# A fused convolution and SiLU layer on one core: one PSUM bank and the hand-written order of work

## The chip, the core and the metric

The kernel runs on one core of a Trainium2 chip. TensorE multiplies, VectorE and ScalarE work element by element, GpSimd (POOL) does small side work, and SyncE (SP) issues most DMAs. Each engine takes its instructions in program order and waits for the others through semaphores. Products land in PSUM, which has eight banks of 512 float32 columns on each of 128 partitions. The metric is device time in microseconds (us), the median of several runs.

## What is computed

```python
w = softmax(weight)                  # 8 heads, 7 taps each
x_pad = zeros of 6 positions, then x # x: 8 x 4096 x 192, float32
a[b, s, h, :] = sum over k of w[h, k] * x_pad[b, s + k, h, :]
h = a @ w_in                         # 32768 x 192 times 192 x 2048
g = h / (1 + exp(-h))                # SiLU
out = g @ w_out                      # 2048 x 192
```

All operands are float32. A float32 matmul here is two passes: every matmul of the program shows as two weight loads and two matmuls in the trace.

## The kernel before

**Blocks and phases.** The 32768 positions are cut into 32 blocks of 1024 (two halves of 512, which lie on partitions 0 to 63 and 64 to 127). Block 0 is computed plainly (`up_plain`, `down_plain`). From block 1 on, both matrix products use fewer multiplications: sums and differences of operands and of results stand in for some products. A steady block has a P phase (the first product, 75 matmuls of 64x128x512 and the plain chunk) and a D phase (the second product, 48 slots of four 128x32 matmuls each). In the D phase of one block, VectorE prepares the convolution of the next; in its P phase VectorE and ScalarE mostly combine what TensorE has just written.

**The order is a list.** `PLAN` holds the order of all work of one steady block as tokens; `step` turns each into instructions, all pinned to program order, so each engine runs its own tokens in the order of the list. A bar only separates TensorE's tokens. A leading `-` means the previous block, `=` the one before it, `+` the next. `START` is the same for the first blocks, and `finish` ends the last. The tokens, as kind, number, dot, group or index:

- `Pr.g` (TensorE, `product`, L625): product r of group g. It runs in half B of the array (partitions 64 to 127) for r in `ON_B` (0, 1, 2, 4, 5, 6, 11, 14, but not r 14 of group 4), otherwise in half A. The two halves run side by side.
- `L.nk` (TensorE, `plain`, L642): the plain chunk, which is computed without the trick. n = 0 is one product per k, on half A, into one bank. n = 1 is a half-width product on each half, into two banks.
- `Di.je` (TensorE, `out_slot`, L741): slot i of the second product; i = 5 is a quarter as wide. It needs SiLU results and, for i of 2 to 5, the differences t of the same j.
- `u`, `X`, `a`, `b`, `S` (`sums_h`): what reads and combines the chains, below. u and S are on ScalarE (L674, L686), X, a and b on VectorE (L668). `SL` is the plain chunk's SiLU (ScalarE, L691).
- `t.ji` (VectorE, `sum_g`, L709): differences of SiLU results; t.01 needs S3.0 and S1.4, t.03 needs t.01.
- `y`, `x`, `z` (ScalarE copies of accumulator parts, L799, L804, L807) and `M` (VectorE sums, L819): they merge the accumulators of the D phase. `o` transposes (VectorE, L829) and `st` stores (SP).
- for the next blocks: `ld` loads (SP), `i` transposes (VectorE, L464), `ha` sets the halo (POOL copy and two SP DMAs), `v.ki` is tap i of the convolution (ScalarE for i = 0, L495, else VectorE, L498), `sp` spreads it by DMA (SP), `w` forms sums of it (VectorE, L532 and L535).

**Chains and banks.** Within a group, products pile up in three banks, and the partial sums in between are results too, so each must be read before the next product of its chain may be added:

```python
CHAINS = ((5, 2, 6, 1, 0, 14), (3, 9, 7, 4, 8), (12, 10))
QUEUE = (0, 4, 1, 2, 3)
CHAIN_BANKS = ((0, 1, 7, 1, 0), (2, 3, 2, 3, 2), (4, 4, 4, 4, 4))
ACC = (7, 1, 3, 5, 6, 4, 0)
PLAIN_BANKS = (7, 7, 3)
```

The first chain is read after products 5, 2, 6, 1, 0 by u5, u4, u2, u0, u1 and at its end by S3. The second is read after 3, 9, 7, 4, 8 by X2, X4, a5, a1, a0, the third after 12 and 10 by b1 and b5. `CHAIN_BANKS` gives the bank of chain and place of the group in `QUEUE`: the third chain is always in bank 4. X2 and X4 write banks 5 and 6, to which P13 and P11 add. In the D phase `ACC` gives the banks: D0 is in bank 7, D1 in 1, D2 in 3, D3 in 5, D4 in 6, D5 in 4 (read by the four x2 copies). `PLAIN_BANKS` gives the plain chunk's: L.0 whole in bank 7, the first half of L.1 in bank 7 as well, its second half in bank 3; SL.0, SL.1 and SL.2 read them in this order.

So L.1 can begin only when SL.0 has read L.0. VectorE's M1 and ScalarE's y2 read one accumulator (D2's bank), M2 and y1 another (D1's), M3 and x0 (D3's), M4, M5 and x1 (D4's) likewise, the sums on partitions 0 to 95 and the copies on 96 to 127.

Of the kernel before, what the change touches and what calls it, by code (L numbers as in the profile page):

```python
# [17 lines left out]
def kernel(  # L18
# [88 lines left out]
    START = (
        "=dp.37 =v.20 =v.00 =dp.19 =v.10 =dp.5 =dp.10 =dp.42 =dp.36 =dp.27 =dp.44 =dp.14 "
        "=dp.8 =dp.12 =dp.38 =dp.28 =dp.22 =dp.25 =dp.43 =dp.26 =dp.45 -ld.2 =dp.30 =dp.3 "
        "=dp.20 -ld.1 =dp.33 =dp.11 -ld.0 =dp.6 =v.01 =dp.17 =v.21 =dp.15 =v.02 =dp.18 =v.11 "  # L110
        "=v.03 =dp.16 =v.12 =dp.47 =v.04 =dp.0 =v.22 =v.13 =dp.23 =v.05 =dp.32 =v.14 =dp.34 "
        "=v.06 =dp.7 =v.15 =sp.0 =v.23 =dp.21 =v.16 =dp.4 =v.24 =sp.1 =dp.40 =v.25 =dp.39 "
        "=v.26 =go.2 =dp.31 -i.2 =sp.2 =dp.1 -i.1 -i.0 =dp.9 -ha.0 =dp.13 =dp.46 =dp.35 =w.0 "
        "-v.20 =dp.41 -v.10 =w.1 =dp.2 -v.11 =w.2 -L.01 -P5.0 -v.21 -L.00 -P5.4 -u5.0 =w.3 "
        "-L.02 -P2.0 -v.22 -v.12 =dp.24 -u4.0 -v.23 -v.00 =dp.29 -SL.0 =w.5 -u5.4 -P6.0 -P3.0 "
        "=cp.1 =cp.2 -P2.4 -u2.0 -X2.0 -L.12 -u4.4 -L.10 -v.01 =cp.0 -L.11 -P9.0 -P1.0 =o.0 "
        "-SL.2 -P13.0 -P6.4 -u0.0 -X4.0 -v.13 -P3.4 -P0.0 -u2.4 =w.4 -S2.0 -P12.0 -P11.0 "
        "-SL.1 -X2.4 -u1.0 -P7.0 -P5.1 -S4.0 -b1.0 -P9.4 -P1.4 -a5.0 -u5.1 -v.14 -P4.0 -P10.0 "
# [24 lines left out]
        "a5.4 S4.4 P5.2 P3.1 b1.4 u2.1 P4.4 P10.4 u5.2 X2.1 v.16 P2.2 P9.1 a1.4 sp.1 P1.1 "
        "P13.1 u4.2 b5.4 X4.1 P8.4 P6.2 u0.1 +i.1 S1.0 P7.1 P0.1 a0.4 u2.2 S2.1 +i.0 P2.3 "
        "P12.1 u1.1 a5.1 +ha.0 P3.2 P1.2 b1.1 P4.1 u0.2 X2.2 P10.1 u4.3 P11.1 a1.1 P9.2 S0.4 "
        "-M7.0 P6.3 S4.1 P8.1 b5.1 P0.2 u2.3 P13.2 X4.2 +v.20 a0.1 P7.2 P11.2 u1.2 -o.0 S2.2 "
        "P3.3 P1.3 S0.1 a5.2 S4.2 P14.1 P12.2 X2.3 +v.10 u0.3 P9.3 P4.2 b1.2 P10.2 P0.3 X4.3 "
        "P11.3 P7.3 u1.3 b5.2 S0.0 a1.2 P12.3 P14.3 S5.0 a5.3 S1.4 P13.3 -o.2 S3.1 P4.3 b1.3 "
        "S3.3 P8.2 P14.2 a1.3 P10.3 t.00 +v.21"
    )  # L150
    QUEUE = (0, 4, 1, 2, 3)
    CHAIN_BANKS = ((0, 1, 7, 1, 0), (2, 3, 2, 3, 2), (4, 4, 4, 4, 4))

    def pin(ins):
        return tc.keep_in_program_order(ins)
# [37 lines left out]
    x0 = x.flatten_outer_dims()[TB - pad : TB, :].rearrange("t (k c) -> c k t", k=NK)  # L193
# [357 lines left out]
    def rows(t, e):  # L551
        return t[R * e : R * e + R]
# [82 lines left out]
    def plain(b, n, k):  # L635
# [3 lines left out]
        for e in range(2) if n else (0,):  # L639
            cols = slice(e * TB // 2, (e + 1) * TB // 2) if n else slice(0, TB)  # L640
            pin(
                nc.tensor.matmul(  # L642
                    banks[PLAIN_BANKS[n and 1 + e]][:, cols],
                    rows(wr[j] if own == e else ws[j], e)[:, a, k, :],
# [43 lines left out]
    def silu_plain(b, i):  # L688
        cols = slice((i - 1) * TB // 2, i * TB // 2) if i else slice(0, TB)
        h = h_of(b, None, int(i > 0))[:, cols]  # L690
        pin(nc.scalar.activation(h, banks[PLAIN_BANKS[i]][:, cols], AF.Silu))  # L691

# [418 lines left out]
```

## Time and profile before

| what | value |
|---|---|
| median of 3 runs | 2359.12 us (2358.9 to 2359.2) |
| the profiled execution, its own time | 2359.21 us |
| its span, first to last instruction | 2357.4 us, granted TensorE clock 0.999 |
| VectorE and ScalarE busy | 2110.6 us and 1179.4 us |
| one L625 matmul as recorded | 589 ns; its weight load 187 ns |
| one X, a or b on VectorE (L668) | 670 to 690 ns |
| one u on ScalarE (L674) | 589 ns |
| one t on VectorE (L709) | 1220 ns |
| HBM traffic | 31.46 MB read, 25.17 MB written |

[...]The distance between starts tells the pace. Times of single tokens are read off the timeline by counting each engine's instructions along the list, in a block whose D phase begins at 1156.38 us.

### The profile page before, as it was taken

Reading aid. Unit: us, or ns where it says so; the run is one execution under the profiler, and the core shown is the slowest. Engines: PE = TensorE matmul, PEld = TensorE weight load, DVE = VectorE, ACT = ScalarE, POOL = GpSimd, SP = SyncE. Lnnn points to the kernel's source line nnn. Section 1 sums busy time; section 2 is a strip of 40 time slices with the busy share of each in tenths; the row PEclk is TensorE's granted clock in tenths of the full one; section 3 lists DMA queues with packets and bytes.
Section 4 is the critical chain, followed back from the end, with each engine's and each line's share of the span. In section 5 each row is a group of like instructions: output and inputs, shape, how many; then the busy total and the mean of one; then the engine's idle time right before and its main releaser. Section 6 shows DMA issues by size and latency. Waiting matters only on the chain.

```text
span 2357.4 us, 43991 instructions
## 1 busy us (share of the span) xinstructions
PE 2349.2 (100%) x17630; PEld 1043.8 (44%) x17630; DVE 2110.6 (90%) x2877; ACT 1179.4 (50%) x2275; POOL 105.7 (4%) x168
## 2 busy tenths in 40 slices
PE   9999999999999999999999999999999999999998
PEld 4344443444444444444444444444444444444444
DVE  8999989899899999998998999999999989899867
ACT  5345644456544465444564445654446644456443
POOL 4910000000000000000000000000000000000000
PEclk9999999999999999999999999999999999999999
DMA  7232111222112221222221122212222112222111
GB/s 158 51 66 52 37 35 35 52 53 47 26 33 52 53 53 29 38 40 52 53 43 28 35 53 52 52 23 36 48 52 52 36 32 37 52 53 39 21 20 28
DMA packets 451245, 106.56 MB, mean 45 GB/s; under 512 B 423584, under 2 KB 428704, under 8 KB 451040
## 3 DMA queue, kind: packets, MB, share of 16 engines
q1 hardware_dynamic: 447392, 101.78, 23.7%
q8 instruction: 138, 2.26, 0.4%
q0 software_dynamic: 448, 1.58, 0.3%
q10 hardware_dynamic: 3200, 0.39, 0.1%
q14 instruction: 67, 0.55, 0.1%
HBM read 31.46 MB, written 25.17 MB: 24 GB/s over the span
## 4 chain that ended last, share of the span: by engine, by line
PE 99%; DVE 1%; ACT 0%; issue 0%; ACTq 0%; DVEq 0%
PE ps L741 47%; PE ps L625 45%; PE ps L642 2%; PE ps L762 2%; PE ps L570 2%; PE ps L1010 1%; PE ps L422 0%; DVE t L709 0%; DVE g L668 0%; DVE cmb L819 0%; DVE cmb L162 0%; ACT u L162 0%; ACT yx L804 0%; DVE osb L162 0%; DVE win L532 0%
## 5 line engine op out<-in xcount | busy, mean ns | idle before, releaser
L741 PE MATMUL ps<-g,wo 128*32 128x512 f32 x2976 | 691.9, 592 | 0.0
L625 PE MATMUL ps<-win,wr 64*128 64x512 f32 x1550 | 691.3, 595 | 0.0
L625 PE MATMUL ps<-win,ws 64*128 64x512 f32 x1550 | 674.3, 603 | 0.6 <-ACT u L674 0.6
L674 ACT COPY u<-ps 128x512 f32<-128x512 f32 x775 | 445.8, 589 | 184.6 <-PE ps L625 158.0
L741 PE MATMUL ps<-t,wo 128*32 128x512 f32 (+2 forms) x4528 | 536.6, 446 | 0.5 <-DVE t L709 0.5
L741 PE MATMUL ps<-t,wx 128*32 128x512 f32 x2976 | 495.7, 592 | 0.0
L625 PE MATMUL ps<-dup,wr 64*128 64x512 f32 x868 | 423.8, 590 | 0.0
L498 DVE SCALAR_TENSOR_TENSOR nat<-xt,taps,nat 128x512 f32<-128x512 f32 x564 | 415.4, 755 | 5.6 <-ACT nat L495 2.0
L709 DVE TENSOR_TENSOR t<-g 128x1024 f32<-128x1024 f32 x248 | 299.9, 1220 | 61.1 <-PE ps L741 41.0
L709 DVE TENSOR_TENSOR t<-g,t 128x1024 f32<-128x1024 f32 x248 | 302.7, 1221 | 30.0 <-PE ps L741 24.7
L625 PEld LDWEIGHTS ps<-win,wr 64*128 64x128 f32 x1550 | 261.4, 186 | 148.3 <-issue 62.4
L686 ACT ACTIVATE g<-ps 128x512 f32<-128x512 f32 x465 | 275.4, 602 | 83.8 <-PE ps L625 78.0
L668 DVE TENSOR_TENSOR g<-u,ps 128x512 f32<-128x512 f32 x465 | 305.7, 673 | 10.1 <-PE ps L625 1.4
L741 PEld LDWEIGHTS ps<-t,wo 128*32 128x32 f32 x4528 | 185.4, 110 | 274.2 <-issue 270.6
L625 PEld LDWEIGHTS ps<-win,ws 64*128 64x128 f32 x1550 | 242.6, 185 | 144.8 <-issue 49.5
L625 PE MATMUL ps<-dup,ws 64*128 64x512 f32 x682 | 280.9, 602 | 0.0
L668 DVE TENSOR_TENSOR ps<-u,ps 128x512 f32<-128x512 f32 x310 | 214.5, 692 | 69.8 <-PE ps L625 64.0
L686 ACT ACTIVATE g<-g 128x512 f32<-128x512 f32 x465 | 268.4, 633 | 15.3 <-DVE g L668 15.3
L804 ACT COPY yx<-ps 32x512 f32<-32x512 f32 x150 | 84.2, 579 | 380.0 <-PE ps L741 377.6
L741 PE MATMUL ps<-g,wx 128*32 128x512 f32 x1488 | 246.0, 594 | 0.0
L741 PEld LDWEIGHTS ps<-g,wo 128*32 128x32 f32 x2976 | 170.1, 110 | 112.5 <-issue 103.9
L807 ACT COPY cmb<-ps 96x512 f32<-96x512 f32 x30 | 17.5, 583 | 403.8 <-PE ps L741 403.8
(90 smaller groups left out, 1849.2 us busy)
## 6 DMA issues: line engine op xcount, KB each, us to landing
dup<-nat SPq DMA_DIRECT2D x345, 128.0 KB, 2.3
nat<-in_x_dram SPq DMA_DIRECT2D x382, 64.0 KB, 2.4
out_dram<-osb SPq DMA_DIRECT2D x376, 64.0 KB, 2.0
raw<-in_moe_w_out_dram SPq DMA_DIRECT2D x8, 384.0 KB, 3.6
raw<-in_moe_w_in_dram SPq DMA_DIRECT2D x12, 192.0 KB, 4.5
ws<-wr POOLq DMA_DIRECT2D x8, 192.0 KB, 5.0
raw<-in_moe_w_in_dram SPq DMA_DIRECT2D x6, 128.0 KB, 3.0
xt<-xt SPq DMA_DIRECT2D x31, 4.5 KB, 1.9
```

What stands on the lines that cost most here:

```text
L498: nc.vector.scalar_tensor_tensor(out=dst, in0=src, scalar=tap, in1=dst, op0=ALU.mult, op1=ALU.add)
L570: nc.tensor.matmul(hs[a, n, e], rows(wr[j], e)[:, a, k, :], rows(d, e)[:, n, k, :], start=k == 0, stop=k == NK - 1,)
L625: nc.tensor.matmul(to[:, cols], raw(g, *LEFT[e][r], e), rhs[:, cols], start=first, stop=True, skip_group_check=True,)
L642: nc.tensor.matmul(banks[PLAIN_BANKS[n and 1 + e]][:, cols], rows(wr[j] if own == e else ws[j], e)[:, a, k, :], rows(dups[b], e)[:, SLOT[e ...
L668: pin(nc.vector.tensor_tensor(out_, u, v, op=op))
L674: pin(nc.scalar.copy(us[b, g, o][:, cols], t1[:, cols]))
L686: pin(nc.scalar.activation(h, src, AF.Silu))
L709: pin(nc.vector.tensor_tensor(t[i // 2][:, i % 2, :], u, v, op=ALU.subtract))
L741: nc.tensor.matmul(accs[b][at][SQ * q : SQ * q + SQ, to], lhs[:, e, SQ * k : SQ * k + SQ], rhs[:, e, ts(q, TB // 4) if i == 5 else to], st ...
L762: nc.tensor.matmul(banks[DOWN_BANKS[k]][R * n : R * n + R, :], wo[j][:, a, e, R * k : R * k + R], gs[b, j, a][:, n, e, :], start=j == 0 an ...
L804: pin(nc.scalar.copy(to, acc[3 * (name[0] == "x") + k][n:P, :]))
L1010: nc.tensor.matmul(by_pe[k][n], rows(diag, n)[:, k, i, :], rows(xts[0], n)[:, k, i : i + TB], start=i == 0, stop=i == K - 1,)
```

## The change

One entry of `PLAIN_BANKS` changes: the first half of L.1 goes to bank 4, the third chain's bank, in place of bank 7; the definition moves up beside the other banks. `PLAN` and `START` hold the same tokens in another order. In the new order L.1's three products are spread among L.0's, the y, z and x copies stand in other places against the M sums, and o, st, ld, i, ha, sp and v stand elsewhere too. No instruction is added or removed. The whole of `PLAN` follows, and of `START` the places where block 0 ends and the first P and D phases meet.

```diff
@@ -79,77 +79,78 @@
 
 
     PLAN = (
-        "P5.0 | -P8.3 -S3.2 -sp.2 v.00 -t.01 | -D1.31 -S2.3 -S5.2 | -D1.01 -a0.2 -S1.3 =st.2 "
-        "-a0.3 -S1.1 | -D1.11 -b5.3 -S0.2 | -D0.00 -S5.4 v.22 -sp.0 -S4.3 | -D2.01 -t.03 "
-        "-S5.1 -S1.2 | -D0.20 =st.0 -t.02 -S0.3 | -D1.21 -S5.3 v.01 | -D2.00 v.11 | -D5.01 "
-        "+ld.0 | -D0.30 v.02 | -D3.00 -t.10 | -D0.01 +ld.1 v.23 | -D0.31 v.24 | -D4.00 -t.11 "
-        "+ld.2 | -D3.01 -w.0 | -D4.01 | -D0.11 -t.13 | -D2.11 -w.1 | -D5.00 | -D4.11 -t.12 | "
-        "-D5.11 | -D2.10 -t.20 | -D4.10 -t.21 | -D5.10 | -D0.21 | -D0.10 -t.23 | -D3.11 "
-        "-z1.0 v.25 u5.0 | -D4.20 v.03 | -D1.10 -t.22 | -D3.10 | -D4.21 -t.30 | -D1.20 v.12 "
-        "| -D2.20 -t.31 | -D2.21 | -D1.30 -t.32 | -D3.21 -t.33 | -D5.20 | -D2.31 v.04 | "
-        "-D1.00 v.26 | -D4.31 -w.2 | -D2.30 v.05 | -D5.30 -y2.0 | -D3.20 v.06 -y1.0 -M1.0 | "
-        "-D3.31 v.13 | -D3.30 -M2.0 | -D5.31 v.14 -x0.0 | -D4.30 -y0.0 -M3.0 | -D5.21 -x1.0 "
-        "| P2.0 | L.00 -M4.0 -x2.1 -w.3 | L.01 | P5.4 u4.0 -w.4 | L.02 | P6.0 u5.4 v.15 | "
-        "P3.0 | P2.4 SL.0 v.16 u2.0 | L.12 -x2.3 X2.0 | L.11 -x2.2 u4.4 | L.10 -M5.0 | P9.0 "
-        "| P1.0 +i.0 SL.2 SL.1 | P13.0 | P6.4 +i.1 -x2.0 u0.0 X4.0 | P3.4 | P5.1 u2.4 +i.2 "
-        "S2.0 | P7.0 | P0.0 -M6.0 +ha.0 X2.4 | P12.0 | P11.0 u1.0 a5.0 u5.1 | P9.4 | P1.4 "
-        "b1.0 S4.0 | P13.4 | P4.0 u0.4 X4.4 -w.5 | P10.0 | P2.1 a1.0 | P0.4 | P7.4 u4.1 b5.0 "
-        "S2.4 | P11.4 | P8.0 -o.1 u1.4 a5.4 | P6.1 | P12.4 S4.4 a0.0 | P14.4 | P14.0 -M7.0 "
-        "u2.1 S0.0 b1.4 | P4.4 | P3.1 S3.4 +v.10 | P10.4 | P1.1 X2.1 S3.0 a1.4 | P5.2 | P9.1 "
-        "u0.1 | P0.1 | P13.1 u5.2 X4.1 | P2.2 b5.4 | P8.4 -o.3 | P7.1 | P5.3 u4.2 a0.4 -st.3 "
-        "u1.1 | P6.2 | P12.1 S2.1 a5.1 u5.3 | P11.1 | P3.2 -st.1 b1.1 u2.2 S5.0 | P4.1 | "
-        "P10.1 X2.2 S4.1 sp.1 | P2.3 S1.0 | P9.2 a1.1 -o.0 | P1.2 | P8.1 u4.3 X4.2 | P6.3 | "
-        "P13.2 u0.2 a0.1 +v.20 | P11.2 b5.1 | P7.2 u2.3 -o.2 S2.2 | P0.2 | P3.3 S4.2 a5.2 | "
-        "P1.3 | P12.2 u1.2 X2.3 | P4.2 u0.3 | P9.3 b1.2 S0.4 | P14.1 | P10.2 S1.4 X4.3 | "
-        "P0.3 S3.1 | P7.3 b5.2 | P11.3 u1.3 a1.2 | P12.3 S0.1 a5.3 | P14.3 | P13.3 +v.21 | "
-        "P4.3 S3.3 b1.3 | P8.2 a1.3 | P10.3 | P14.2 t.00"
+        "+ld.1 P5.0 | -P8.3 -S1.4 -a0.2 -S4.3 | -D0.00 -t.01 -S0.2 | -D1.00 -S1.2 =o.2 v.00 "
+        "| -D2.01 -t.03 -S5.1 =st.2 | -D2.00 -b5.3 | -D1.20 -sp.0 v.21 -S5.3 | -D4.01 u5.0 "
+        "-t.02 -S1.3 | -D5.01 -sp.2 | -D4.00 -t.10 | -D0.20 -t.11 | -D3.01 | -D0.11 -t.12 | "
+        "-D1.30 v.22 | -D3.00 +ld.2 -t.13 | -D2.11 -a0.3 | -D5.00 | -D2.10 -t.20 -S0.3 | "
+        "-D3.11 v.11 | -D5.10 | -D4.11 -w.0 | -D0.30 v.12 | -D4.10 -t.21 | -D1.11 -t.23 | "
+        "-D0.21 | -D0.01 v.23 -w.1 | -D3.10 -t.22 | -D5.21 | -D0.31 | -D5.11 | -D1.10 -t.30 "
+        "| -D1.01 -t.31 | -D2.20 | -D2.21 v.13 | -D5.20 | -D4.21 v.01 v.14 | -D4.20 v.24 | "
+        "-D1.21 -w.2 | -D3.20 -t.33 | -D2.30 v.02 | -D1.31 -t.32 | -D2.31 -y1.0 | -D5.30 "
+        "v.03 | -D0.10 v.25 | -D3.21 -z1.0 v.15 -y0.0 | -D4.31 -y2.0 -w.3 | -D5.31 -M1.0 | "
+        "-D3.30 -x2.1 v.26 -x2.0 | -D4.30 -x2.2 -M2.0 | -D3.31 -w.5 -x0.0 -M3.0 | L.02 | "
+        "P2.0 -x2.3 -w.4 | P5.4 | P3.0 u4.0 -M6.0 | L.12 v.16 u5.4 | L.00 | P6.0 -x1.0 -M4.0 "
+        "| L.10 u2.0 | P2.4 | L.01 X2.0 | L.11 v.04 u4.4 | P9.0 | P1.0 SL.0 -M5.0 SL.2 | "
+        "P6.4 | P13.0 u0.0 X4.0 SL.1 | P5.1 | P3.4 -M7.0 S2.0 +i.2 u2.4 | P0.0 | P7.0 X2.4 | "
+        "P11.0 | P12.0 u1.0 a5.0 -o.1 | P9.4 | P1.4 S4.0 b1.0 -st.1 u5.1 | P13.4 | P4.0 X4.4 "
+        "u0.4 | P10.0 | P2.1 a1.0 +ld.0 v.05 | P7.4 | P0.4 u4.1 b5.0 | P14.0 | P8.0 u1.4 "
+        "v.06 S5.0 | P11.4 | P14.4 a5.4 S3.0 a0.0 S2.4 | P6.1 | P12.4 S3.4 | P4.4 | P3.1 "
+        "u2.1 b1.4 S4.4 | P5.2 | P10.4 X2.1 | P1.1 a1.4 u5.2 | P9.1 b5.4 | P2.2 u0.1 | P8.4 "
+        "X4.1 | P5.3 u4.2 | P7.1 a0.4 | P0.1 +i.1 u5.3 sp.1 | P12.1 a5.1 | P6.2 u1.1 | P3.2 "
+        "-o.0 | P4.1 u2.2 b1.1 | P13.1 | P2.3 a1.1 | P10.1 S2.1 | P1.2 u4.3 X2.2 | P8.1 | "
+        "P11.1 -o.3 u0.2 | P13.2 S1.1 a0.1 | P6.3 S4.1 | P9.2 +i.0 | P0.2 b5.1 u2.3 +ha.0 | "
+        "P3.3 S0.0 X4.2 | P1.3 S2.2 | P12.2 u1.2 | P11.2 X2.3 | P7.2 u0.3 b1.2 | P14.1 S4.2 "
+        "| P9.3 a5.2 S0.4 | P0.3 -st.0 | P10.2 S1.0 X4.3 | P14.2 u1.3 | P7.3 b5.2 +v.20 "
+        "-st.3 | P4.2 S0.1 | P12.3 a5.3 S3.1 | P14.3 +v.10 a1.2 | P13.3 | P4.3 S5.2 b1.3 | "
+        "P8.2 S2.3 | P11.3 a1.3 S3.3 | P10.3 S5.4 t.00 S3.2"
     )
     START = (
-        "=dp.37 =v.20 =v.00 =dp.19 =v.10 =dp.5 =dp.10 =dp.42 =dp.36 =dp.27 =dp.44 =dp.14 "
...
-        "-v.20 =dp.41 -v.10 =w.1 =dp.2 -v.11 =w.2 -L.01 -P5.0 -v.21 -L.00 -P5.4 -u5.0 =w.3 "
-        "-L.02 -P2.0 -v.22 -v.12 =dp.24 -u4.0 -v.23 -v.00 =dp.29 -SL.0 =w.5 -u5.4 -P6.0 -P3.0 "
...
+        "=dp.28 =v.20 =v.10 =dp.44 =v.00 =dp.18 =dp.6 =dp.40 =dp.7 =dp.32 =dp.23 =dp.30 "
...
+        "=v.26 =go.2 =sp.0 =dp.19 -i.0 =dp.46 -i.2 =dp.31 -ha.0 =dp.9 =sp.2 =dp.4 =dp.41 "
+        "-v.10 -v.00 -v.11 =dp.8 -v.20 -v.01 =dp.5 -v.12 =dp.16 -v.02 =w.0 =dp.10 =w.1 =cp.0 "
+        "-L.01 -P5.0 -v.03 =cp.1 -L.02 -P5.4 =w.2 -u5.0 -L.10 =w.3 -u5.4 -P2.0 -P3.0 -v.13 "
...
+        "-b1.3 -S5.1 ld.0 -S4.3 -t.01 -D0.01 -S5.2 -D0.21 -t.02 -D1.11 -sp.0 -a5.3 -D1.10 "
+        "-v.25 -t.03 -P8.2 P5.0 +ld.1 -P4.3 -P10.3 -D1.30 -b5.3 -v.26 -D1.00 -a0.2 -sp.2 "
...
+        "-D5.11 -D2.10 u5.0 -t.20 -D0.20 -w.1 -D3.11 -t.21 -D4.10 -w.2 -D2.11 -t.23 -P8.3 "
+        "P2.0 -D0.31 -a0.3 -t.22 -D3.10 -S0.3 -S1.3 -D4.21 v.21 -S5.3 u4.0 v.01 -D4.20 -t.30 "
...
+        "P13.3 -o.3 P4.3 S3.2 b1.3 -st.3 +v.10 P8.2 +v.20 a1.3 P10.3 P11.3 S5.2 t.00 S2.3"
     )
     QUEUE = (0, 4, 1, 2, 3)
     CHAIN_BANKS = ((0, 1, 7, 1, 0), (2, 3, 2, 3, 2), (4, 4, 4, 4, 4))
+    PLAIN_BANKS = (7, 4, 3)
 
     def pin(ins):
         return tc.keep_in_program_order(ins)
@@ -599,7 +600,6 @@
     X_OF = {13: 0, 10: 5, 5: 3, 11: 4, 14: 1}
     CHAINS = ((5, 2, 6, 1, 0, 14), (3, 9, 7, 4, 8), (12, 10))
     ACC = (7, 1, 3, 5, 6, 4, 0)
-    PLAIN_BANKS = (7, 7, 3)
     XBANK = {2: 5, 4: 6}
```

## The prediction

> **What bounds the kernel now.** I read the page's busy times and its chain that ended last, then the waits, then single blocks through windows and timeline.
>
> ```profile
> PE 2349.2 (100%) x17630; PEld 1043.8 (44%) x17630; DVE 2110.6 (90%) x2877; ACT 1179.4 (50%) x2275; POOL 105.7 (4%) x168
> ...
> PE 99%; DVE 1%; ACT 0%; issue 0%; ACTq 0%; DVEq 0%
> ```
>
> TensorE is the chain. Whether it runs at its pace, its busy share can't say, so I compare starts. The windows below are one steady block: D phase, P phase, whole block.
>
> ```profile
> 1156.38:1192.60 36.22, 36.22 (x386) 12.09 (x385) 33.06 (x39) 9.51 (x19) 0.00 (x0) 1.00 0.30 52
> 1192.60:1228.76 36.16, 36.16 (x173) 20.04 (x169) 32.63 (x52) 27.36 (x54) 0.63 (x1) 1.00 0.18 34
> ...
> 1156.38:1228.76 72.38, 72.38 (x554) 32.13 (x553) 65.70 (x90) 36.86 (x72) 0.63 (x1) 1.00 0.24 43
> ```
>
> The columns are length, then busy time of PE, PEld, DVE, ACT, POOL, then clock and DMA. The block's 72.38 recurs to 0.01 us from the third block to the last, so a gain or loss per block counts some 29 times. In the P phase each half of the array (A: partitions 0 to 63, B: 64 to 127) has 39 full products of two passes, and passes of one half start 0.4292 us apart (1208.75 and 1209.18 below), and six half-width ones at 0.2155: 33.48 + 1.29 = 34.77. The phase takes 36.16, so 1.39 is lost: 0.10 at the switch to D, 1.29 in stalls on half A (about 1.2 on B, side by side with them). The D phase has no stalls: its starts run at 0.858 per slot, 0.218 for a quarter-width one. Which stalls they are:
>
> ```profile
> DVE cmb L819 <- ACT yx L804: 29.7, 88, 3.0
> ...
> PEld ps L642 <- ACT g L691: 17.9, 30, 0.7
> ```
>
> The second row is L.12, which shares bank 7 with L.0 and waits for SL.0, once a block:
>
> ```profile
> 1195.54 0.60 ACT L691 ACTIVATE g<-ps 128x512 f32<-128x512 f32 x1 [0.29 <-PE ps L625]
> ...
> 1196.19 0.18 PEld L642 LDWEIGHTS ps<-dup,ws 64*128 64x128 f32 x1 [0.59 <-ACT g L691]
> 1196.19 0.48 PE L642 MATMUL ps<-dup,ws 64*128 64x256 f32 x1
> ...
> 1196.51 0.38 PE L642 MATMUL ps<-dup,ws 64*128 64x256 f32 x1
> ```
>
> Silu ends at 1196.14, weights load at 1196.19, the second pass comes 0.32 later in place of 0.2155. With 0.05 at the first pass that is 0.15 us on half A. The other kind, P3.1 -> X2.1 -> P9.1:
>
> ```profile
> 1208.75 0.59 PE L625 MATMUL ps<-dup,ws 64*128 64x512 f32 x1
> ...
> 1209.07 0.70 DVE L668 TENSOR_TENSOR ps<-u,ps 128x512 f32<-128x512 f32 x1 [0.59 <-PE ps L625]
> 1209.18 0.59 PE L625 MATMUL ps<-dup,ws 64*128 64x512 f32 x1
> ...
> 1209.82 0.69 PE L625 MATMUL ps<-win,ws 64*128 64x512 f32 x1
> ...
> 1210.35 0.83 PE L625 MATMUL ps<-win,ws 64*128 64x512 f32 x2
> ```
>
> Half A's passes of P10.4 start at 1208.75 and 1209.18, so P9.1 was due at 1209.61. It may not add to its bank before X2.1 has read it (ends 1209.77): start 1209.82, and its second pass 0.53 later, not 0.43: 0.31 lost. In the same way P10.1 loses 0.26 (behind b1.1), P9.3 0.26 (X2.3), P7.3 0.20 (X4.3). With 0.10 at the first product and L.12's 0.15 that is half A's 1.29 (0.10 + 0.15 + 0.31 + 0.26 + 0.26 + 0.20).
>
> **The rule in it.** From a product's start to the start of its VectorE reader 1.13 us pass, the reader takes 0.69, and 0.05 go to the weight load: 1.87. With one product of the same half between, 1.72 are offered: 0.15 late, and 0.105 for a second pass whose weights could not load beneath the first. That is 0.26. A ScalarE copy (1.06 + 0.59 + 0.05 = 1.70) is just in time and costs only about 0.09, as P6.2, P6.3 and P14.3 show (0.08 each). With two between (2.58) nothing is lost. The block's stalls obey: lost = reader's end + 0.05 + 0.105 - due start, if positive. One more kind: P14.2 loses 0.41 on B because its weight load stands in TensorE's queue behind that of P10.3, which waits for b1.3; a wait on one half can hold up the other.
>
> **The Trainium skill.** "Trainium Kernel Development and Optimization", Performance Expectations, calls matmul busy time "a bad metric" because matmuls are pipelined; the trace agrees (72.38 of 72.38 busy with 1.4 lost). "TensorE: Matmul & The Clock Gate", Part 3, has weight loads overlap running matmuls on other row groups, and be pulled ahead; the halves' matmuls starting 0.01 apart and the exposed 0.105 after a waited load agree. "PSUM — Partial Sum Buffer", PSUM bank collisions, wants engines kept apart by bank and 32-partition quadrant. Copies (partitions 96 to 127) and sums (0 to 95) already wait for each other here (29.7 us above); no run shows a collision. "TensorEngine Tiling (Array Packing)", Key Properties, says that a change of tiling mode drains TensorE; the trace shows 0.09 to 0.2 at each.
>
> **The change part by part.** Counts of every instruction stay; only places and one bank move.
>
> *Bank of L.1's first half.* SL.0 -> L.12 goes: 0.15 on A, 0.04 on B. New are x2 -> L.12 and SL.1 -> P12.0, both on bank 4. x2.3, the last x2, stands on ScalarE behind x0.0 (0.58) and ends some 0.9 us after the last D's results, about 0.8 before L.12 is due. SL.1 ends about 1.2 before P12.0. Both cost nothing. If that cover went, L.12 would delay both halves one for one, with everything behind it on TensorE.
>
> *Links on half A.* With one product of the half between I count 15 links before and 10 after. After, on A: P10.4 behind b1.4, P7.1 behind X4.1, P7.3 behind X4.3, at 0.26 each; P14.4 behind u1.4, 0.09; P9.1 behind X2.1 nothing, since the 0.26 just lost at P10.4 makes its 1.72 into 1.98. P8.1, P8.2 and P8.3 follow P4 of the other half, and A lags B by more than 0.3 there: nothing. With 0.10 at the first product, 0.97. Several readers end within 0.1 of the point (X2.1, b5.2 before P12.3, X2.2 before P13.2, a1.2 before P8.2); I put 0.05 for them: 1.02.
>
> *Half B:* 0.10, P2.2 0.09, P4.1 0.03, P1.3 0.09, and one new wait: P5.0 reopens bank 0, which S3.3 must have read. ScalarE from the start of P0.3: 1.06, u1.3 0.49, v.20 0.62, S0.1 0.52, S3.1 0.52, v.10 0.62, S5.2 0.52, S2.3 0.52, S3.3 0.60 (starts follow at these distances in the trace), together 5.47, and 0.155 to the array: 5.62. Six products of B offer 5.15: 0.47 lost. B's 0.78 stay 0.2 below A's, so A decides. Queued behind P5.0 is only P8.3, then D.
>
> *The seam into D.* S1.4, three Silus after S3.3, ends 7.04 after P0.3's start, t.01 (1.22) at 8.30, D2.01 is due at 8.49: 0.1 us of room, cost nothing. In the list before, S1.4 ran long before t.01.
>
> *Moved on SP, POOL and VectorE.* The halo (ha.0, POOL 0.59, DMA issue 0.62, 1.9 to landing) moves from P0.0 to P0.2; its taker v.20 starts 4.7 us after i.0 ends, 1.6 of room. It passes st.1, ld.0 and sp.1 on SP, all issued earlier. o.2 and st.2 move into the D phase; t.10 takes a buffer that st.2 must have left, and t.10 has 2 us of room. VectorE's D-phase work is 31 us of 36. M3 still stands right behind x0, M4 behind x1: VectorE goes on waiting there, about 0.9 us under D, with X2.0 still done 0.2 before P9.0. So avoiding common reads is worth nothing on TensorE.
>
> *START.* The two products slots dp.24 and dp.29 no longer interrupt the first P phase (two switches, some 0.45 saved); a second stretch of P tokens stands within the first D phase (some 0.25 added). Its other stalls I can't price; the first blocks of the trace lose some 5 us over the steady pace, so +-2.5 is taken, value -0.2.
>
> *Sum.* (1.29 - 1.02) x 29 = 7.8, and 0.2: 8.0 less. The profiled execution is 2359.21 (span 2357.4 and 1.8 around it; 0.1 above the median): **2351.2**.
>
> **Rivals.**
> - *Even (0.22).* The near misses count in full: four on A at up to 0.1. 0.97 + 0.35 is 1.32, as before: 2359. For it: P6.0, P6.2 and P14.3 paid 0.08 with readers done 0.02 ahead. Against: P2.4, 0.05 ahead, paid half.
> - *More gained (0.15).* Stalls of one half hide beneath the lag of the other, as P9.2 and P10.2 show today (one between, nothing lost). If two of the three 0.26 go so: 0.5 per block, 2344.5.
> - *Slower (0.18).* ScalarE's tail at the seam. Late by over 0.2 us there, half B ends last, and D2.01 waits behind t.01 too; beyond 0.2 each us counts, and past 0.45 the gain is gone. At 0.7 the block is 0.23 longer: 6.7 more, 2365.9. For it: eight copies and Silus in a row, ScalarE 27 of 36 us busy in this phase, a halo DMA moved close before v.20. Against: no link in that row waited for in my count.
> - That the change doesn't do what it says: VectorE's waits for copies would remain near 29.7 us. They lie under TensorE; the time stays that of the forecast.
>
> **How the numbers follow.** Forecast 0.45, own range 2347 to 2354.4. About 0.2% (4.7 us) is what can be told from no change. Forecast and more-gained: faster, 0.60. Even: 0.22. Slower: 0.18. Range 2343 to 2365: beneath it the far end of more-gained, above it half of slower.
>
> **What would show it.** Right: block period 72.1, P phase 35.9; no wait of L642 on ACT g L691; P10.4, P7.1 and P7.3 late by 0.26; P5.0 waiting for S3.3 about 0.5 without TensorE's D phase starting later. Wrong: D2.01 behind t.01, half B ending last, or L.12 waiting for a copy of bank 4.

## The result and the profile after

| | before | after |
|---|---|---|
| median of 6 runs each, on one chip | 2359.18 us (2358.9 to 2359.48) | 2349.12 us (2348.82 to 2349.58) |
| ratio after to before, 95% interval | | 0.9957 (0.9945 to 0.997) |
| the profiled execution and its span | 2359.21, 2357.4 | 2349.19, 2347.5 |
| start of the third D phase, from which the blocks are steady | 215.51 | 212.43 |
| from there to the start of the last D phase, 29 blocks | 2098.87 | 2092.12 |
| from there to the end | 43.04 | 42.93 |

Faster by 10.06 us, 0.43%. The spans differ by 9.9: 3.08 come from the first blocks, 6.75 from the steady ones (0.233 in each) and 0.11 from the end.

The page's busy times and the chain that ended last, after:

```profile
PE 2340.3 (100%) x17630; PEld 1061.0 (45%) x17630; DVE 2099.6 (89%) x2877; ACT 1187.3 (51%) x2275; POOL 96.8 (4%) x168
...
PE 99%; DVE 0%; ACT 0%; issue 0%; ACTq 0%
```

TensorE is the whole chain, as before, and the two lines don't tell the kernels apart. The windows of one steady block do (D phase, P phase, block; columns: length, busy time of PE, PEld, DVE, ACT, POOL, clock, DMA share, GB/s):

```profile
1150.31:1186.53 36.22, 36.22 (x386) 12.07 (x385) 33.09 (x40) 8.14 (x17) 0.00 (x0) 1.00 0.20 40
1186.53:1222.45 35.92, 35.92 (x172) 20.62 (x168) 32.19 (x50) 29.01 (x55) 0.19 (x1) 1.00 0.27 47
1150.31:1222.45 72.14, 72.14 (x553) 32.69 (x552) 65.28 (x90) 37.15 (x72) 0.19 (x1) 1.00 0.24 43
```

The D phase has its 36.22 still. All of the gain is in the P phase, 36.16 to 35.92. What was waited for, after (engine, tile, line, releaser: total us, times, longest):

```profile
PEld ps L642 <- issue: 69.4, 218, 0.8
DVE cmb L819 <- ACT yx L804: 61.6, 59, 4.2
PEld ps L625 <- DVE ps L668: 57.8, 214, 0.8
...
PEld ps L625 <- ACT u L674: 15.6, 61, 0.6
```

L642's wait for ACT g L691, L.12 behind SL.0, is gone. VectorE's wait for the copies has doubled, from 29.7 to 61.6: both lists keep a copy and a sum of one accumulator apart by letting the second wait for the first, M1 for y2 (1.21 us in this block) and M3 for x0 (0.77).

The product that lost 0.15 before, L.12, in the timeline of after:

```profile
1187.92 0.19 PEld L642 LDWEIGHTS ps<-dup,ws 64*128 64x128 f32 x1 [0.23 <-issue]
...
1188.35 0.38 PE L642 MATMUL ps<-dup,ws 64*128 64x256 f32 x1
...
1188.57 0.38 PE L642 MATMUL ps<-dup,ws 64*128 64x256 f32 x1
```

Its weights load 0.43 ahead of the first pass, and the second pass comes 0.22 after the first: nothing lost. One of the links that remain, b1.4 -> P10.4:

```profile
1202.10 0.69 DVE L668 TENSOR_TENSOR u<-u,ps 128x512 f32<-128x512 f32 x1 [0.64 <-PE ps L625]
...
1202.84 0.29 PEld L625 LDWEIGHTS ps<-dup,ws 64*128 64x128 f32 x2
1202.84 0.69 PE L625 MATMUL ps<-dup,ws 64*128 64x512 f32 x1
...
1203.38 0.59 PE L625 MATMUL ps<-dup,ws 64*128 64x512 f32 x1
```

b1.4 ends at 1202.79, the weights load at 1202.84 (0.15 late), and the second pass comes 0.54 after the first in place of 0.43: 0.25 lost. And the new wait on half B, S3.3 -> P5.0:

```profile
1219.99 1.08 ACT L686 ACTIVATE g<-ps 128x512 f32<-128x512 f32 x2
...
1221.12 0.18 PEld L625 LDWEIGHTS ps<-dup,wr 64*128 64x128 f32 x1 [0.29 <-ACT g L686]
1221.12 0.69 PE L625 MATMUL ps<-dup,wr 64*128 64x512 f32 x1
```

The first row is S2.3 and S3.3; S3.3 ends at 1221.07. P5.0 starts 0.05 later and had been due 0.29 earlier; with its exposed second load it loses 0.395. D starts at 1222.45 all the same, since half A ends 0.28 after B.

What each product of this block lost, in us (its distance from the one before it of its half, less 0.4292 a pass):

| half | predicted | measured |
|---|---|---|
| A | first 0.10, P14.4 0.09, P10.4 0.26, P9.1 0, P7.1 0.26, P7.3 0.26, near misses 0.05: 1.02 | first 0.104, P9.0 0.047, P14.4 0.127, P10.4 0.254, P9.1 0.011, P7.1 0.265, P7.3 0.262: 1.07 |
| B | first 0.10, P2.2 0.09, P4.1 0.03, P1.3 0.09, P5.0 0.47: 0.78 | first 0.105, P1.0 0.047, P2.2 0.081, P1.3 0.081, P4.3 0.077, P5.0 0.395: 0.79 |

### The profile page after: what moved, and what is told of

It is laid out like the page before. It is cut to its first block, busy times and chain, and to the rows that moved or that the text cites. A ratio compares the mean times of both kernels' runs of the same rounds, so it can differ in the third digit from the quotient of the medians.

```text
span 2347.5 us, 43988 instructions
## 1 busy us (share of the span) xinstructions
PE 2340.3 (100%) x17630; PEld 1061.0 (45%) x17630; DVE 2099.6 (89%) x2877; ACT 1187.3 (51%) x2275; POOL 96.8 (4%) x168
## 4 chain that ended last, share of the span: by engine, by line
PE 99%; DVE 0%; ACT 0%; issue 0%; ACTq 0%
PE ps L741 47%; PE ps L625 42%; PE ps L642 5%; PE ps L762 2%; PE ps L571 2%; PE ps L1010 1%; PE ps L423 0%; DVE t L709 0%; ACT g L686 0%; DVE cmb L163 0%; ACT u L163 0%; DVE osb L163 0%; DVE osb L829 0%; DVE g L668 0%; PE ps L449 0%
## 5 line engine op out<-in xcount | busy, mean ns | idle before, releaser
L625 PE MATMUL ps<-win,wr 64*128 64x512 f32 x1550 | 720.3, 597 | 0.0
L741 PE MATMUL ps<-g,wo 128*32 128x512 f32 x2976 | 702.4, 593 | 0.0
L625 PE MATMUL ps<-win,ws 64*128 64x512 f32 x1550 | 631.3, 595 | 0.0
L741 PE MATMUL ps<-t,wo 128*32 128x512 f32 (+2 forms) x4528 | 545.7, 446 | 0.0
L625 PE MATMUL ps<-dup,wr 64*128 64x512 f32 x868 | 425.4, 593 | 0.0
L686 ACT ACTIVATE g<-g 128x512 f32<-128x512 f32 x465 | 286.1, 633 | 231.5 <-DVE g L668 231.5
L625 PEld LDWEIGHTS ps<-win,wr 64*128 64x128 f32 x1550 | 275.6, 186 | 150.4 <-issue 67.8
L668 DVE TENSOR_TENSOR g<-u,ps 128x512 f32<-128x512 f32 x465 | 311.2, 680 | 28.8 <-PE ps L625 14.6
L625 PE MATMUL ps<-dup,ws 64*128 64x512 f32 x682 | 324.2, 599 | 0.0
L625 PEld LDWEIGHTS ps<-win,ws 64*128 64x128 f32 x1550 | 254.7, 186 | 110.5 <-issue 40.8
L686 ACT ACTIVATE g<-ps 128x512 f32<-128x512 f32 x465 | 266.8, 597 | 41.1 <-PE ps L625 38.4
L668 DVE TENSOR_TENSOR ps<-u,ps 128x512 f32<-128x512 f32 x310 | 214.7, 692 | 43.7 <-ACT g L686 19.0
L741 PEld LDWEIGHTS ps<-t,wx 128*32 128x32 f32 x2976 | 120.5, 110 | 217.5 <-issue 202.3
```

Of the source, the lines that this page charges most:

```text
L625: nc.tensor.matmul(to[:, cols], raw(g, *LEFT[e][r], e), rhs[:, cols], start=first, stop=True, skip_group_check=True,)
L668: pin(nc.vector.tensor_tensor(out_, u, v, op=op))
L686: pin(nc.scalar.activation(h, src, AF.Silu))
L741: nc.tensor.matmul(accs[b][at][SQ * q : SQ * q + SQ, to], lhs[:, e, SQ * k : SQ * k + SQ], rhs[:, e, ts(q, TB // 4) if i == 5 else to], st ...
```

## The experiments

All are lists of the same tokens, or shorter readers, on this kernel. Each ran beside before on one chip; "period" is the usual length of a steady block, 72.375 before and 72.142 after. The lists there take a few lines fewer, so the same code stands up to three lines higher: the L625 of after is L622 or L623, its L668 L665 or L666, and so on.

### The bank alone, in the old order

```diff
-L.00 -M4.0 -x2.1 -w.3 | L.01 | P5.4 u4.0 -w.4 | L.02 | P6.0 u5.4 v.15
+L.00 -M4.0 -x2.1 -x2.0 -w.3 | L.01 | P5.4 u4.0 -x2.2 -w.4 | L.02 | P6.0 u5.4 -x2.3 v.15
...
-L.12 -x2.3 X2.0 | L.11 -x2.2 u4.4
+L.12 X2.0 | L.11 u4.4
...
-PLAIN_BANKS = (7, 7, 3)
+PLAIN_BANKS = (7, 4, 3)
```

The copies of bank 4 go ahead of L.12, in START cp.0 too. In block 1 SL.1 reads after P12.0 has added to its bank, so that block's plain chunk holds other values; no instruction is added or left out.

> The list of before with the new bank alone; the four x2 copies (and, in the first block, one copy of the plain second product) come ahead of L.12, since they read bank 4. Theory (the bank removes SL.0 -> L.12, 0.15 us per block on half A and 0.04 on half B; A falls from 1.29 to 1.14 of stalls, B stays at 1.16): the block 0.12 to 0.15 shorter, 4 us less, 2355 (2354 to 2356). Rival (the gain is the list's alone): 2359.2 within 0.6.

Measured: 2359.71 us, ratio 1.0002 (0.9993 to 1.0011). The forecast of a gain fell. L.12 lost nothing any more, as it said, yet the period is 72.338, only 0.037 less. The timeline shows the next link of the same half, X2.1 -> P9.1:

```profile
1282.43 0.69 DVE L665 TENSOR_TENSOR ps<-u,ps 128x512 f32<-128x512 f32 x1 [0.63 <-PE ps L622]
...
1283.17 0.29 PEld L622 LDWEIGHTS ps<-win,ws 64*128 64x128 f32 x2
1283.18 0.69 PE L622 MATMUL ps<-win,ws 64*128 64x512 f32 x1
```

P9.1 starts 0.05 after X2.1 (1283.12) and loses 0.35 where it lost 0.31 before; P9.0, which lost nothing before, loses 0.08 behind X2.0. So of the 0.15 that L.12 gave back, 0.12 are lost later on half A, at readers that did not come earlier. At the rate of 0.037 the 29 blocks bring 1.1 us. Against this the third D phase starts 0.55 later (216.06), and four blocks (those that end at 360.87, 650.58, 867.93 and 1012.76 us) take 0.13, 0.36, 0.34 and 0.16 more, because VectorE starts one add 0.35 late in each; the last of these experiments comes back to such starts. The bank alone is worth nothing that can be measured; the gain needs the new order. That order in turn needs the bank: it puts L.12 ahead of L.00, and in bank 7 the two products would lie on the same columns.

### The start of before, under the new list

```diff
-a1.3 P10.3 t.00 +v.21
+a1.3 S5.2 S2.3 P10.3 S5.4 t.00 S3.2 +v.21 S1.1 -st.0
```

The new PLAN and bank; START is the old one, with cp.0 ahead of L.12, and closes with the tokens that the new PLAN expects to be done (the diff is against the old START). Block 1's plain chunk is changed as in the run above.

> The changed kernel with the first blocks' list of before, which is closed with the few tokens that the new steady list wants done. Theory (the two traces stand 3.1 us apart when the third D phase begins, and that is kept to the end): 2352.2 (2351.5 to 2353). Rival (what START gains or loses is made up by the blocks behind it): 2349.1 within 0.6.

Measured: 2353.77 us, ratio 0.9977 (0.9968 to 0.9986), 0.8 above the range of the forecast; the rival falls. The period is 72.142, the new one; the difference from after, 4.6 us, is in the first blocks: the third D phase starts at 216.28, and that block takes 0.43 more, where the two lists join. One later block (it ends at 433.49 us) takes 0.35 more, again with one VectorE add that starts 0.35 late (413.99). The old START on its own costs 3.08 (215.51 to 212.43); the other 0.77 up to the third D phase and the 0.43 go with the way it was joined to the new list. Later blocks make up for none of it.

### Half B's new wait taken away

```diff
-P4.3 S5.2 b1.3 | P8.2 S2.3 | P11.3 a1.3 S3.3
+P4.3 S3.3 S5.2 b1.3 | P8.2 S2.3 | P11.3 a1.3
```

> The changed kernel with S3.3 moved ahead of S5.2 and S2.3 on ScalarE, so that P5.0 need not wait (0.40 us lost on half B in the trace of after). Theory (half A ends 0.28 later than B and decides): no change, 2349.1 within 0.7, with P5.0's wait gone in the trace. Rival (ScalarE's tail at the seam decides): up to 0.3 to 0.4 per block, 2338 to 2341.

Measured: 2349.03 us, ratio 0.9956 (0.9941 to 0.9971), period 72.141. P5.0 loses nothing now, and the block is no shorter: half A sets the end of the P phase.

### One more product between P12.4 and P10.4

```diff
-P14.4 a5.4 S3.0 a0.0 S2.4 | P6.1 | P12.4 S3.4
+P12.4 a5.4 S3.0 a0.0 S2.4 | P6.1 | P14.4 S3.4
```

On top of the run before.

> As S3.3 early, and P14.4 and P12.4 exchanged on half A, which gives both links P0.4 -> P14.4 and P12.4 -> P10.4 one more product between. Theory: P14.4's 0.13 and P10.4's 0.25 go, but P9.1, no longer sheltered, pays 0.26: 0.12 to 0.13 less per block on A, while B may lose 0.1 at P5.2 (S3.4 is later) out of its room of over 0.6: 2345.5 (2344 to 2347). Rival (stalls on one half simply move on along it): 2349 within 0.7.

Measured: 2351.95 us, ratio 0.9969 (0.9957 to 0.998): slower than after, above the forecast and above its rival. P14.4 loses nothing now, but the period is 72.246. The timeline:

```profile
1275.29 0.60 ACT L684 ACTIVATE g<-ps 128x512 f32<-128x512 f32 x1 [0.49 <-PE ps L623]
...
1275.94 0.18 PEld L623 LDWEIGHTS ps<-dup,wr 64*128 64x128 f32 x1 [0.70 <-ACT g L684]
1275.94 0.69 PE L623 MATMUL ps<-dup,wr 64*128 64x512 f32 x1
1275.94 0.18 PEld L623 LDWEIGHTS ps<-dup,ws 64*128 64x128 f32 x1
1275.94 0.69 PE L623 MATMUL ps<-dup,ws 64*128 64x512 f32 x1
```

S3.4 follows P14.4 and ends at 1275.89; P5.2 of half B waits for it. The weight load of P10.4 (the one with ws, half A) stands right behind P5.2's in TensorE's queue, so P10.4 starts in the same hundredth and loses 0.149, though b1.4 is long done. P9.1 is then without the shelter that the prediction gave it (0.26 lost just ahead of it) and loses 0.343 in place of 0.011. P7.1 and P7.3 stay at 0.263 each. Half A: 0.10 more, as the period says.

### Shorter readers, on the tight links and on others

```diff
+    SHORT = (("b1", 4), ("X2", 1), ("X4", 1), ("X4", 3), ("b5", 2))
...
-            pin(nc.vector.tensor_tensor(out_, u, v, op=op))
+            n = TB // 2 if (name, g) in SHORT else TB
+            pin(nc.vector.tensor_tensor(out_[:, 0:n], u[:, 0:n], v[:, 0:n], op=op))
```

The five sums named read half their columns. The second kernel names b1.3, X2.3, X4.0, X4.4 and b5.0, which have room. The Trainium skill ("VectorE: DVE Perf Modes", the section on the TRN2 errata) gives (N + 151)/0.96 ns for a float32 add of N columns, which it checked at 512 and 2048; for 256 that is an estimate of 0.42 us. The trace has 0.43 (X4.3, which reads one operand from PSUM), against 0.69 for 512.

> The changed kernel with five VectorE sums (b1.4, X2.1, X4.1, X4.3, b5.2) made on columns 0 to 255 alone, so part of the chains' combination is left out; each stands in a link of half A with one product between. Theory (the link's length is the stall): 0.27 us off each reader, half A's three stalls of 0.26 go, A ends ahead of B, and B (0.74 of stalls, 0.40 of it at P5.0) decides: 0.2 to 0.33 per block, 2339 to 2343. Rival (VectorE's load or TensorE's own pace sets the phase): the same as for the five sums outside tight links, whichever that is.

> The changed kernel with five VectorE sums (b1.3, X2.3, X4.0, X4.4, b5.0) made on columns 0 to 255 alone, so part of the chains' combination is left out; each has two products of its half between. The same time is taken from VectorE as in the run with the tight ones. Theory: nothing, 2349.1 within 0.7. Rival (VectorE's load): as much as the tight ones give, 6 us or more.

Measured: tight 2338.06 us, ratio 0.991 (0.9895 to 0.9925), a little more gained than forecast, period 71.787; loose 2348.65 us, ratio 0.9955 (0.994 to 0.997), period 72.146. VectorE had the same work taken away in both. On five links it brings 0.36 us a block, 11 us in all; elsewhere nothing. So VectorE's load (89% busy in after) is not the bound: single readers are. On half A 0.70 is left of 1.07. Two links that half A's lag behind B had sheltered now show, P8.1 with 0.15 and P8.2 with 0.08. P8.3 loses 0.19 for another reason: it starts 0.01 after P5.0 of half B (1215.67 and 1215.66 us), which waits for S3.3 and whose weight load stands ahead of P8.3's. Half A now ends only 0.01 after B.

### Both together: the tight readers short, S3.3 early

> The five short sums in tight links together with S3.3 early; the same part of the combination is left out. Theory (the later half decides): A's stalls and B's P5.0 are both gone, B has 0.35 and A about 0.3 left, though P8.1, P8.2 and P8.3, which follow products of half B, may now be late on A: 0.45 to 0.7 per block, 2328 to 2336, more than the short sums and S3.3 early give one by one. Rival (effects add up one by one): the time of the short sums within 1 us.

Measured: 2338.06 us, ratio 0.991, no less than with the short readers alone. The forecast fell: this is the rival's number. The windows (D phase, P phase) show where the gain went:

```profile
1216.85:1253.26 36.41, 36.41 (x385) 11.95 (x384) 33.55 (x41) 8.61 (x18) 0.00 (x0) 1.00 0.20 39
1253.26:1288.63 35.37, 35.37 (x172) 20.12 (x168) 30.39 (x50) 28.55 (x55) 0.19 (x1) 1.00 0.27 47
```

The P phase is 0.19 shorter than with the short readers alone (35.56): P5.0 no longer waits, and P8.3's 0.19 is gone with it. The D phase is 0.19 longer than its 36.22. In the timeline of that D phase:

```profile
1217.49 1.22 DVE L709 TENSOR_TENSOR t<-g,t 128x1024 f32<-128x1024 f32 x1
...
1218.77 0.12 PEld L741 LDWEIGHTS ps<-t,wx 128*32 128x32 f32 x3 [0.90 <-DVE t L709]
```

D2.01 waits for t.01, the wait that the prediction's slower rival named. t.01 starts at 0.64 after the D phase's begin, behind a0.2 (which ends at 0.63) and S1.4 (0.60), that is, behind the tails of both VectorE and ScalarE. In after it ends 0.34 before D2.01 starts; here TensorE came to it 0.55 earlier in the block, and the tails did not. That is the next bound: of the 0.55 that the P phase is shorter, 0.36 per block is kept with these tails.

### Sums ahead of copies

```diff
--w.5 -x0.0 -M3.0 | L.02
+-w.5 -M3.0 -x0.0 | L.02
...
-P6.0 -x1.0 -M4.0 | L.10
+P6.0 -M4.0 -x1.0 | L.10
```

> The changed kernel with M3 ahead of x0 and M4 ahead of x1, so that ScalarE's copy waits for VectorE's sum of the same accumulator in place of the other way round. Theory (these waits lie under other work; x2.3 ends just in time for L.12): 2349.1 to 2350. Rival (the order of copies and sums on one accumulator is what the new list gains by): 2 us or more slower.

Measured: 2371.15 us, ratio 1.005 (1.0034 to 1.0067), period 72.877: the largest miss. The D phase is unchanged, P9.0 loses 0.74 and P1.0 0.57. The timeline around P9.0, first of after, then of this run:

```profile
1189.22 0.58 ACT L804 COPY yx<-ps 32x512 f32<-32x512 f32 x1
...
1189.88 0.59 ACT L674 COPY u<-ps 128x512 f32<-128x512 f32 x1
...
1190.57 0.68 DVE L668 TENSOR_TENSOR ps<-u,ps 128x512 f32<-128x512 f32 x1
...
1191.30 0.30 PEld L625 LDWEIGHTS ps<-win,ws 64*128 64x128 f32 x4 [0.18 <-DVE ps L668]
```

```profile
1199.70 0.58 ACT L802 COPY yx<-ps 32x512 f32<-32x512 f32 x1 [0.74 <-DVE cmb L817]
...
1200.30 1.26 ACT L672 COPY u<-ps 128x512 f32<-128x512 f32 x2
...
1200.92 0.70 DVE L666 TENSOR_TENSOR ps<-u,ps 128x512 f32<-128x512 f32 x1 [1.26 <-ACT u L672]
...
1201.67 0.30 PEld L623 LDWEIGHTS ps<-win,ws 64*128 64x128 f32 x4 [0.70 <-DVE ps L666]
```

Top to bottom they are x1, u2.0, X2.0 and P9.0's (and P1.0's) weight loads. M4 comes late on VectorE, behind w.4, M6 and v.16; x1 now waits 0.74 for it on ScalarE, u2.0 stands behind x1, X2.0 needs u2.0, P9.0 needs X2.0. The swap of two readers costs this much only through what is queued behind the one that waits.

### Sums ahead of copies, with nothing behind the copies

```diff
--D4.30 -x2.2 -M2.0 | -D3.31 -w.5 -x0.0 -M3.0 | L.02 | P2.0 -x2.3 -w.4 | P5.4 | P3.0 u4.0 -M6.0 | L.12 v.16 u5.4 | L.00 | P6.0 -x1.0 -M4.0 | L.10 u2.0
+-D4.30 -x2.2 -x2.3 -M2.0 | -D3.31 -w.5 -M3.0 | L.02 | P2.0 -w.4 | P5.4 | P3.0 u4.0 -M4.0 -x0.0 | L.12 -M6.0 u5.4 | L.00 | P6.0 v.16 | L.10 u2.0 -x1.0
```

> The new list, with the sums M3 and M4 ahead of the copies x0 and x1 again, but so that nothing urgent stands behind a waiting copy: x2.3 stands right after x2.2, x0 behind u4.0, x1 behind u2.0, and on VectorE M4 comes before M6 and v.16. Theory (what cost 0.73 us per block in the run with the sums first was that u4.0, u2.0 and x2.3 stood behind copies that waited for M3 and M4, and X2.0 behind u2.0; the order of the readers itself costs nothing): P9.0 starts on time again, as X2.0 then starts 0.03 after u2.0, ends about 40.87 after the block's first D start and P9.0 is due at 41.05; the 0.047 that P9.0 and P1.0 lose each in the new list go too. Half A then loses 1.02, period 72.10, 0.047 x 29 = 1.4 less: 2347.7 (2347.2 to 2349.3). VectorE's wait for copies falls from 61.6 to about 40. Rival (reading one bank with two engines in this order costs by itself, whatever is queued behind): the period stays above 72.3 and the time above 2353.

Measured: 2349.37 us, ratio 0.9958 (0.9945 to 0.9972). The period is 72.097: P9.0 and P1.0 lose nothing, the 0.047 is won, and VectorE waits 38.1 us for copies in place of 61.6. So the order of readers costs nothing by itself, and the rival falls. The total is that of after nevertheless: four of the 29 blocks, those that end at 428.8, 1943.3, 2015.8 and 2232.4 us, take 0.34 to 0.37 more, together 1.4 us, as much as the others win. VectorE's instructions of the first of these blocks, b1.4 and X2.1, and then those of the block after it:

```profile
408.12 0.69 DVE L666 TENSOR_TENSOR u<-u,ps 128x512 f32<-128x512 f32 x1 [0.64 <-PE ps L623]
...
409.33 0.69 DVE L666 TENSOR_TENSOR ps<-u,ps 128x512 f32<-128x512 f32 x1 [0.52 <-ACT g L684]
...
480.57 0.69 DVE L666 TENSOR_TENSOR u<-u,ps 128x512 f32<-128x512 f32 x1 [0.63 <-PE ps L623]
...
481.43 0.70 DVE L666 TENSOR_TENSOR ps<-u,ps 128x512 f32<-128x512 f32 x1 [0.17 <-PE ps L623]
```

X2.1 starts 1.21 after b1.4, not 0.86, while TensorE and ScalarE ran to the hundredth as in the other blocks up to there. The releaser named there, a Silu, is no later than elsewhere. In the other three blocks it is b1.4, X4.1 and X4.3 that start late. Two more lists asked whether this goes with the place of single instructions.

### The same with S3.3 early, and with v.16 ahead of M6

```diff
-P4.3 S5.2 b1.3 | P8.2 S2.3 | P11.3 a1.3 S3.3
+P4.3 S3.3 S5.2 b1.3 | P8.2 S2.3 | P11.3 a1.3
```

```diff
-L.12 -M6.0 u5.4 | L.00 | P6.0 v.16
+L.12 v.16 u5.4 | L.00 | P6.0 -M6.0
```

> The list of the run with the sums first and the copies later (period 72.097 in 25 of 29 blocks, and in four blocks 0.35 us more, where one VectorE instruction behind P12.4 to P9.1 starts 0.35 late with no releaser of its own in the trace), with S3.3 also ahead of S5.2 as in the run that moved it alone. Theory (the four late starts are not a wait in the list: they belong to how the instruction stream happens to lie, and moving one ScalarE instruction by two places may shift or drop them): period 72.10 in most blocks, fewer or other blocks with the 0.35: 2347.8 if none (2347.6 to 2349.3). Rival (they come from the new order of sums and copies itself, through some wait): the same four blocks again, 2349.3.

> The same list with the sums first and the copies later, but on VectorE v.16 before M6, as in the new list. All of VectorE's work up to X2.0 ends at the same time, so no wait changes. Theory (the late starts belong to the instruction stream): period 72.10 in most blocks, the 0.35 in other blocks or in none: 2347.8 if none (2347.6 to 2349.3). Rival (a wait of this order): the same four blocks, 2349.3.

Measured: 2349.28 us, ratio 0.9957 (0.9944 to 0.9971), and 2348.99 us, ratio 0.9957 (0.9944 to 0.9969). Both have the period of 72.09 to 72.10 and the same four longer blocks, as the rival said for this order. So the late starts are not chance and did not move with these two tokens.

The rival's reason does not follow, for lists without this order have such starts too: the bank alone in its four longer blocks (335.31, 636.31, 860.80 and 1010.97 us), the start of before in one (413.99), and after itself, where adds at 632.10 and 2135.03 us start 0.37 and 0.28 late and no block is longer for it. The traces show one thing that all of these have in common. The profile has a DMA queue that it calls "q14 instruction", with 67 packets in a whole run, and one of its packets begins 0.65 to 0.95 us after each of these late starts: at 409.99, 1923.78, 1998.93 and 2227.00 us in the run with nothing behind the copies, where the adds start at 409.33, 1922.97, 1998.27 and 2226.34. That fetching instructions is what holds VectorE is not shown, as no run moved these packets; the cause stays open. No list tried that does the whole work is measurably faster than after.

## Why the prediction was right

**What bounds it** held: the shorter readers brought 0.36 us a block on the tight links and nothing elsewhere.

**The bank.** L.12's stall went and its new neighbours cost nothing, as written. What that is worth was not worked out apart from the list; alone, in the old order, it is 0.037 a block, not 0.15, since later links on half A take the rest. In the sum this did no harm: both totals of half A were taken from the whole list.

**The links on half A** came out one for one: P10.4, P7.1 and P7.3 at 0.254 to 0.265 for 0.26, and P9.1, sheltered, at 0.01. P14.4 lost 0.127 for 0.09. The near misses were put at 0.05 and are 0.05, but at another place: P9.0. "X2.0 still done 0.2 before P9.0" was mis-sized. X2.0 ends 0.11 before P9.0 starts, and by the prediction's own rule 0.155 is needed.

**Half B** came out at 0.79 for 0.78, in part by luck: P5.0 lost 0.40 for 0.47, and P1.0 (0.05) and P4.3 (0.08), which were not in the list, made up for it. That A decides is shown by the run with S3.3 early.

**The seam** had more room than the 0.1 written: t.01 ends 0.34 before D2.01 starts. The mechanism of the slower rival is real, though: it stood in the way as soon as the P phase was 0.55 shorter.

**Avoiding common reads** "is worth nothing on TensorE": nearly. The run with nothing behind the copies gains 0.047 a block, with fewer of these waits, and a careless order costs 0.73. The sign that VectorE's waits would tell whether the change does what it says was a poor one: they doubled, while the time fell.

**The sum.** Steady blocks gained 6.75 for the 7.8 written: 0.233 a block for 0.27, as half A lost 1.07 and not 1.02. The term that was mis-sized most is START: 3.08 gained where 0.2 with 2.5 either way was written, so even its margin was too small. The traces show where. The first P phase begins 2.42 later (101.96 for 99.54), as the two product slots dp.24 and dp.29 now stand ahead of it. From there to the second P phase's begin, its own interruptions included, 74.59 us pass in place of 78.21; the second P phase takes 35.88, not 37.76. In before that phase lost 0.87 at P1.0 and L.02, 0.63 at P9.4 and 0.32 at P5.1, and some slots of the D phase ahead of it started late, D4.20 and D2.20 among them; after has none of these. They could have been read off the trace of before, product by product, as those of the steady block were; they were put down as what can't be priced. 7.8 + 0.2 against 6.75 + 3.08 + 0.11: the two errors partly cancel, which is luck, and the time was 2.1 us lower than predicted.

**The rivals.** "Even" asked for the near misses in full: of the four named only X2.1 cost anything, 0.01 at P9.1, and one that was not named paid 0.047 (X2.0). "More gained" asked for two of the three 0.26 to hide: none did. "Slower" asked for the seam, which had room.

## What to carry to other kernels

On an engine that is always busy, subtract its pace from the starts of one steady block and give every lost hundredth to one reader; then price an edit by what the next link on the same half loses once the first is gone, since of the 0.15 of one stall that was taken away alone, 0.12 was lost again further on. When two readers of one bank change places, look at what is queued behind the one that now waits: that cost 0.73 us a block, the order itself nothing. And price the first blocks from the trace as carefully as the steady ones: they held three tenths of this gain.

## What was not expected of the hardware

- A wait on one half of the array holds the other through the order of weight loads alone: P10.4 started with P5.2 in the same hundredth, 0.149 late, with its own operands ready. P8.3 started 0.01 after P5.0 and lost 0.19 in the run with the tight readers short, and nothing once P5.0 no longer waited.
- VectorE starts single adds some 0.35 us late with no releaser in the trace that was late: in the same four of 29 blocks in the four lists with sums ahead of copies, at other places in other lists, and twice in after, where it costs nothing. A packet of the queue "q14 instruction" follows each of those named above within 1 us. Whether it belongs to the cause is open.
